# A sign bit made by another engine: converting 64-bit weights in an attention and gated-MLP kernel

## The chip, the cores and the metric

The kernel runs on one core of one Trainium2 chip, in one launch. The metric is the device time of one execution in microseconds. A core has five engines with a queue each: TensorE (PE in the profile, its weight loads are PEld), VectorE (DVE), ScalarE (ACT), GpSimd (POOL) and SyncE (SP), which issues nearly all DMAs here. An engine works through its queue in order and waits on semaphores.

## The reference

Banded attention with sinks, and then a gated MLP over its output. The attention has 4 batches, 8 heads, 768 positions and head size 64:

```python
scores = scale * np.matmul(q, k.transpose(0, 1, 3, 2))
keep = is_sink | in_window            # key < 4, or 0 <= query - key < 128
a = softmax(np.where(keep, scores, -1e9));  out = np.matmul(a, v)
h = np.maximum(x @ w_in, 0.0)         # x: heads side by side, 512 wide; w_in: 512 x 1024
conv = sum(conv_w[k] * shift(h, k - 1) for k in range(3))     # along positions, per channel
return (h * sigmoid(conv)) @ w_out    # w_out: 1024 x 512
```

q, k and v are 32-bit floats. The three weights w_in, conv_w and w_out are scaled by a 64-bit number when they are made and so arrive as 64-bit floats, which the kernel has to turn into 32-bit ones on the chip.

## The kernel before, in words

Each pair of heads of a batch is a group; there are 16 groups, and a group has six tiles of 128 queries. One step of the main loop (line 734) is one tile: scores (line 378 for the first batch, in plain f32; lines 381 and 382 for the others, as high and low parts), the mask and row minimum on VectorE (line 577), the exponential on ScalarE (line 580), the sum and its reciprocal on VectorE (lines 583 and 584), the scaling of the probabilities on GpSimd (line 586), their transposes on TensorE (line 603 for the first batch), a copy to SBUF by ScalarE, and the product with v (lines 655 and 678). Once three tiles of a half are done, the result goes to the MLP's input as a high and a low part (lines 389 and 390).

The MLP of a batch is cut into units of 256 positions by 128 hidden channels. A unit has twelve products into `ph` (line 204), the gate (lines 211 to 230, on ScalarE, VectorE and GpSimd), and products into `po` (line 239). Units are filled in between the attention steps; the first batch's begin in the middle of its attention, since the MLP needs x.

The weights are loaded in 128x512 tiles: eight of w_in, eight of w_out, and one small tile (24x128) of conv_w, the taps. `WHEN` (line 35) and line 757 convert one tile per step from step 2 to step 18. `load` fetches the raw pairs of 32-bit words; `narrow` makes a 32-bit float of each pair; `split` makes of it a high part H on GpSimd (line 130) and a low part L on VectorE (line 131), as TensorE multiplies in a reduced form of f32. For the taps `narrow` writes into a part of a buffer `hb`, and there is no split.

In `narrow`, ScalarE multiplies the upper word, read as a float, by 2^-112 (line 118), which takes the difference of the two exponent biases out. The result `low` has the sign in its top bit, then three zero bits, then the wanted bits. VectorE shifts it left by 3 (line 121), which drops the sign, or-s in the top three bits of the lower word (line 122), and or-s the sign back in (line 123). `w` and `low` are both of tag `st`, which has three buffers and which the output tiles of line 244 use too. Line 120 lets ScalarE's instruction wait for an exponential of a recent step.

The order of each engine's queue is not written out by hand: the program is traced, and a planner orders it by priority along a timeline of its own with costs it assumes (line 938). The attention steps get a higher priority (line 731), TensorE's instructions of the attention go through `c.pin`, and some waits are added by `follow` (line 47).

Of the kernel before, what the change touches and what calls it, by code (L numbers as in the profile page):

```python
# [14 lines left out]
ALU = mybir.AluOpType  # L15
# [23 lines left out]
def f(ap):  # L39
    return ap.bitcast(F32)  # L40
# [6 lines left out]
def follow(c, ins, other, reason):  # L47
    c.tc.add_manual_dep(ins.ins, other.ins.name, mybir.DependencyInfo(mybir.DependencyClass.Sync, mybir.DependencyReason.DATA),
                        reason=reason)
# [17 lines left out]
class Moe:  # L67
# [41 lines left out]
    def narrow(self, raw, to=None):  # L109


        if raw.dtype == F32:
            return raw
        nc, (rows, n) = self.c.nc, raw.shape[0:2]
        w = self.temp("st", 512, 3)[0:rows, 0:n] if to is None else to
        low = self.temp("st", 512, 3)[0:rows, 0:n]
        lo, hi, wi, li = raw[:, :, 0], raw[:, :, 1], w.bitcast(I32), low.bitcast(I32)
        first = nc.scalar.mul(low, f(hi), 2.0 ** -112)
        if len(getattr(self.c, "exps", [])) > 1:
            follow(self.c, first, self.c.exps[-2], "late")  # L120
        nc.vector.tensor_scalar(wi, li, 3, None, ALU.logical_shift_left)
        nc.vector.scalar_tensor_tensor(out=wi, in0=lo, scalar=29, in1=wi, op0=ALU.logical_shift_right, op1=ALU.bitwise_or)  # L122
        nc.vector.scalar_tensor_tensor(out=wi, in0=li, scalar=-0x80000000, in1=wi, op0=ALU.bitwise_and, op1=ALU.bitwise_or)  # L123
        return w

    def split(self, raw, parts, at):
# [815 lines left out]
```

## Time and profile before

| | |
|---|---|
| runs before | 474.14 us median of 3 (473.42 to 474.23) |
| profiled execution | 473.48 us, of which the span is 471.8 us |
| granted TensorE clock | 0.997 of full speed |
| PE | 444.6 us (94%) |
| PEld | 388.3 us (82%) |
| DVE | 339.0 us (72%), 1190 instructions |
| ACT | 321.3 us (68%) |
| POOL | 281.3 us (60%), 557 instructions |

Busy times are unions over the span, from the first to the last instruction. An average over the span hides that the stages differ: what matters is which engine is full in the stage that a change touches, and what waits for it there. The end of a matmul is modelled, and matmuls are pipelined, so a duration of one of them is longer than the time it takes from the engine.

### The profile page before, as it was taken

How to read it: one execution, taken by the hardware profiler on the slowest of the kernel's cores; microseconds unless marked ns; L12 is line 12 of the kernel's file. 1: busy time of each engine (PE TensorE's matmuls, PEld its weight loads, DVE VectorE, ACT ScalarE, POOL GpSimd, SP SyncE). 2: the span in 40 equal slices, each digit the busy share in tenths (PEclk: the TensorE clock that was granted, in tenths of full speed). 3: DMA queues.
4: the chain of work that ended last, by engine and by line, in shares of the span. 5: the costliest groups of instructions: out<-in, count | busy, mean ns of one | idle time of the engine just before them, and what ended most of it. 6: DMA issues, size and time to landing. Idle time of an engine off the chain costs nothing.

```text
span 471.8 us, 10560 instructions
## 1 busy us (share of the span) xinstructions
PE 444.6 (94%) x3181; PEld 388.3 (82%) x3181; DVE 339.0 (72%) x1190; ACT 321.3 (68%) x1027; POOL 281.3 (60%) x557
## 2 busy tenths in 40 slices
PE   3898989898899999999999999999999999999994
PEld 3576768697798988898989898988989898998982
DVE  4799999758858668786766859685767663665562
ACT  4989957768867868785867767675857654554542
POOL 3474786626858658676755757667656671445340
PEclk9999999999999999999999999999999999999998
DMA  6888674388667472655273655545250101000001
GB/s 140 219 229 251 183 201 107 81 199 203 167 153 179 137 175 68 161 146 133 61 192 81 166 119 134 143 120 124 71 141 15 46 1 46 0 23 24 24 24 53
DMA packets 105851, 55.91 MB, mean 119 GB/s; under 512 B 83072, under 2 KB 98712, under 8 KB 105784
## 3 DMA queue, kind: packets, MB, share of 16 engines
q1 hardware_dynamic: 105640, 55.00, 45.5%
q8 instruction: 28, 0.46, 0.4%
q14 instruction: 39, 0.32, 0.2%
q10 hardware_dynamic: 144, 0.13, 0.1%
HBM read 28.17 MB, written 6.29 MB: 73 GB/s over the span
## 4 chain that ended last, share of the span: by engine, by line
PE 75%; DVE 11%; ACT 4%; POOL 3%; DMA 2%; issue 2%; DVEq 0%; POOLq 0%; ACTq 0%
PE ph L204 26%; PE po L239 25%; PE px L655 7%; PE sc L382 3%; PE sc L381 3%; PE pts L617 3%; PE px L678 2%; DVE stm L122 2%; PE tq L305 1%; PE tk L331 1%; DVE stm L123 1%; DMA kk<-bk 1%; DMA raw<-in_q_dram 1%; DVE roomH L577 1%; DVE roomL L577 1%
## 5 line engine op out<-in xcount | busy, mean ns | idle before, releaser
L239 PE MATMUL po<-woH,g 128*128 128x512 f32 x384 | 138.2, 405 | 1.5 <-POOL g L226 0.8
L204 PE MATMUL ph<-xH,wiH 128*128 128x258 f32 (+1 forms) x384 | 110.7, 288 | 0.0
L204 PE MATMUL ph<-xL,wiH 128*128 128x258 f32 (+1 forms) x384 | 109.6, 286 | 0.0
L204 PE MATMUL ph<-xH,wiL 128*128 128x258 f32 (+1 forms) x384 | 109.1, 284 | 0.0
L226 POOL TENSOR_SCALAR g<-t 128x256 fp32r<-128x256 f32 x94 | 44.3, 472 | 74.5 <-DVE t L219 50.6
L586 POOL TENSOR_SCALAR pe<-pe,sm 128x132 f32<-128x132 f32 (+1 forms) x144 | 62.8, 447 | 37.7 <-DVE sm L584 19.2
L239 PEld LDWEIGHTS po<-woH,g 128*128 128x128 f32 x384 | 69.4, 189 | 13.2 <-POOL g L226 1.7
L227 POOL TENSOR_TENSOR g<-t,g 128x256 fp32r<-128x256 f32 x94 | 74.5, 793 | 5.8
L239 PE MATMUL po<-woL,g 128*128 128x512 f32 x192 | 76.1, 396 | 0.0
L216 DVE SCALAR_TENSOR_TENSOR t<-hb,cw,t 128x256 f32<-128x256 f32 x96 | 53.8, 560 | 29.4 <-ACT t L215 28.9
L204 PEld LDWEIGHTS ph<-xH,wiL 128*128 128x128 f32 x384 | 72.8, 190 | 2.2
L204 PEld LDWEIGHTS ph<-xH,wiH 128*128 128x128 f32 x384 | 72.7, 189 | 2.0
L204 PEld LDWEIGHTS ph<-xL,wiH 128*128 128x128 f32 x384 | 72.7, 189 | 1.6
L580 ACT ACTIVATE pe<-pe,sm 128x132 f32<-128x132 f32 (+1 forms) x144 | 58.2, 406 | 14.4 <-DVE sm L577 12.8
L218 ACT ACTIVATE t<-t 128x256 f32<-128x256 f32 x96 | 40.1, 418 | 36.3 <-DVE t L217 35.9
L219 DVE SCALAR_TENSOR_TENSOR t<-t,hb 128x256 f32<-128x256 f32 x96 | 48.3, 504 | 15.1 <-ACT t L218 14.3
L215 ACT ACTIVATE t<-hb,cw 128x256 f32<-128x256 f32 x96 | 49.0, 511 | 12.4 <-POOL g L227 10.1
L217 DVE SCALAR_TENSOR_TENSOR t<-hb,cw,t 128x256 f32<-128x256 f32 x96 | 54.4, 567 | 4.0 <-POOL pe L586 0.5
L211 ACT ACTIVATE hb<-ph 128x258 f32<-128x258 f32 (+1 forms) x96 | 36.8, 384 | 17.4 <-PE ph L204 13.9
L577 DVE CUSTOM_DVE_ANT_0 pe<-sc,m 128x132 f32<-128x132 f32 (+1 forms) x144 | 39.8, 287 | 7.7 <-PE sc L382 6.9
L381 PE MATMUL sc<-kk,X 128*128 128x260 f32 (+1 forms) x144 | 42.3, 304 | 1.5 <-issue 1.1
L655 PE MATMUL px<-pT,vraw 128*64 128x128 f32 (+1 forms) x512 | 43.0, 317 | 0.0
(161 smaller groups left out, 896.1 us busy)
## 6 DMA issues: line engine op xcount, KB each, us to landing
X<-bq SPq DMA_DIRECT2D x96, 96.0 KB
vraw<-in_v_dram SPq DMA_DIRECT2D x16, 384.0 KB
out_dram<-stm SPq DMA_DIRECT2D x23, 256.0 KB
kk<-kk SPq DMA_DIRECT2D x24, 198.0 KB
raw<-in_k_dram SPq DMA_DIRECT2D x24, 192.0 KB
raw<-in_q_dram SPq DMA_DIRECT2D x24, 192.0 KB
kk<-bk SPq DMA_DIRECT2D x48, 96.0 KB
raw<-in_q_dram SPq DMA_DIRECT2D x16, 96.0 KB
```

The lines of the kernel that those rows point to most:

```text
L204: self.latest = nc.tensor.matmul(u.h[:, 0:W], w[:, cc, ff * P:(ff + 1) * P], x[:, cc, t0:t1], start=(i == 0), stop=(i == len(prods) - 1))
L215: nc.scalar.mul(a, prev, cw[:, 0, ff:ff + 1])
L216: nc.vector.scalar_tensor_tensor(out=e, in0=this, scalar=cw[:, 1, ff:ff + 1], in1=a, op0=ALU.mult, op1=ALU.add)
L217: nc.vector.scalar_tensor_tensor(out=a, in0=nxt, scalar=cw[:, 2, ff:ff + 1], in1=e, op0=ALU.mult, op1=ALU.add)
L219: nc.vector.scalar_tensor_tensor(out=a, in0=e, scalar=1.0, in1=this, op0=ALU.add, op1=ALU.mult)
L227: nc.gpsimd.tensor_tensor(out=u.g[:, 1], in0=a, in1=f(u.g[:, 0]), op=ALU.subtract)
L239: ins = nc.tensor.matmul(po[:, 0:c.DM], u.g[:, a, tt * P:(tt + 1) * P], w[:, ff, :], start=(ff == 0 and i == 0), stop=(ff == NFF - 1 and i ...
L381: self.c.pin(self.nc.tensor.matmul(pc, X[:, j, u, :], kk[:, j, lo:hi], start=True, stop=False))
L577: nc.vector.tensor_tensor_reduce(out=pe[:, j, cols], in0=pc[:, P - at:SW][:, cols], in1=mk, op0=ALU.add, op1=ALU.min, scale=1.0, scalar=3. ...
L580: exp = nc.scalar.activation(pe[:, j, cols], pe[:, j, cols], AF.Exp, bias=sm[:, j:j + 1], scale=-1.0, accum_out=sm[:, 2 + 2 * j:3 + 2 * j])
L586: nc.gpsimd.tensor_scalar(pe[:, j, cols], pe[:, j, cols], sm[:, 8 + j:9 + j], 1.0, ALU.mult, ALU.mult)
L655: ins = nc.tensor.matmul(px[h][D * j:D * j + D, P * at:P * at + n], s.v[:, j, kt, :], pT, start=(h not in open_), stop=False, skip_group_c ...
```

## The change

The product of `low` with zero is a zero with the sign of `low`. GpSimd makes it, into `w`, in place of VectorE's shift. VectorE's first remaining instruction or-s the top three bits of the lower word into `w`, as before; its second shifts `low` left by 3 and or-s the result in.

```diff
         first = nc.scalar.mul(low, f(hi), 2.0 ** -112)
         if len(getattr(self.c, "exps", [])) > 1:
             follow(self.c, first, self.c.exps[-2], "late")
-        nc.vector.tensor_scalar(wi, li, 3, None, ALU.logical_shift_left)
+        nc.gpsimd.tensor_scalar(w, low, 0.0, 1.0, ALU.mult, ALU.mult)
         nc.vector.scalar_tensor_tensor(out=wi, in0=lo, scalar=29, in1=wi, op0=ALU.logical_shift_right, op1=ALU.bitwise_or)
-        nc.vector.scalar_tensor_tensor(out=wi, in0=li, scalar=-0x80000000, in1=wi, op0=ALU.bitwise_and, op1=ALU.bitwise_or)
+        nc.vector.scalar_tensor_tensor(out=wi, in0=li, scalar=3, in1=wi, op0=ALU.logical_shift_left, op1=ALU.bitwise_or)
         return w
```

Before, the order of a tile is ScalarE (118), VectorE (121, 122, 123), GpSimd (130), VectorE (131). After, it is ScalarE (118), GpSimd (121), VectorE (122, 123), GpSimd (130), VectorE (131).

## Rows read from the trace of the kernel before

**Rows 1.** Busy time by stretch: start:end, length, each engine's busy us (and instructions).

```profile
core 0: us, PE busy (x) PEld busy (x) DVE busy (x) ACT busy (x) POOL busy (x), PEclk, DMA share, GB/s
...
12.00:88.00 76.00, 66.40 (x466) 52.35 (x465) 72.19 (x221) 61.31 (x187) 48.36 (x70) 1.00 0.69 187
88.00:100.00 12.00, 11.76 (x99) 10.62 (x99) 6.84 (x23) 9.21 (x27) 5.71 (x11) 1.00 0.68 159
100.00:200.00 100.00, 96.66 (x741) 85.13 (x741) 73.80 (x329) 76.67 (x275) 67.68 (x147) 1.00 0.64 158
200.00:400.00 200.00, 200.00 (x1462) 178.42 (x1461) 140.77 (x518) 136.10 (x452) 128.23 (x259) 1.00 0.41 103
```

**Rows 2.** Chain of waits, 12 to 88 us: shares of this stretch by line.

```profile
by line: DVE stm L122 11.1%; DVE stm L123 8.2%; issue 7.4%; DMA raw<-in_q_dram 6.4%; DVE roomH L577 5.6%; DVE roomL L577 5.4%; DVE woL L131 4.9%; ACT roomL L580 4.6%; DVE stm L121 4.1%; DVE xL L390 3.7%; PE sc L378 3.5%; DVE wiL L131 3.5%; 
```

**Rows 3.** Waits of TensorE, 12 to 88 us: total us, times, longest.

```profile
PE sc L378 <- DVE sm L577: 3.0, 4, 1.1
PE pts L603 <- POOL roomL L586: 1.8, 3, 0.8
PE pts L603 <- POOL roomH L586: 1.1, 2, 0.6
```

**Rows 4.** VectorE by line, 12 to 88 us: count, busy us, mean ns, idle before.

```profile
L123 DVE SCALAR_TENSOR_TENSOR stm<-stm,stm 128x512 int32<-128x512 int32 x16 | 11.7, 732 | 0.0
L121 DVE TENSOR_SCALAR stm<-stm 128x512 int32<-128x512 int32 x16 | 9.6, 598 | 0.5 <-ACT stm L118 0.3
...
L121 DVE TENSOR_SCALAR hb<-stm 24x128 int32<-24x128 int32 x1 | 0.2, 206 | 0.0
```

**Rows 5.** Durations of lines 121 and 123, ns: least, median, most.

```profile
L121 DVE TENSOR_SCALAR stm<-stm x16: 405/540/886, 13.7 to 80.4; 128x512 int32<-128x512 int32 x16
...
L123 DVE SCALAR_TENSOR_TENSOR stm<-stm,stm x16: 664/680/1193, 16.8 to 84.3; 128x512 int32<-128x512 int32 x16
```

**Rows 6.** Timeline of GpSimd and VectorE: start us, us, instruction.

```profile
57.98 0.62 POOL L130 TENSOR_SCALAR wiH<-stm 128x512 fp32r<-128x512 f32 x1 [0.65 <-DVE sm L584]
...
76.86 0.61 POOL L130 TENSOR_SCALAR woH<-stm 128x512 fp32r<-128x512 f32 x1
...
58.00 0.89 DVE L121 TENSOR_SCALAR stm<-stm 128x512 int32<-128x512 int32 x1
58.80 0.41 DVE L577 CUSTOM_DVE_ANT_0 roomL<-sc,roomH 128x260 f32<-128x260 f32 x1
...
76.87 1.14 DVE L122 SCALAR_TENSOR_TENSOR stm<-wo6r,stm 128x512 int32<-128x512 int32 x1
```

**Rows 7.** Chain of waits in order of time: start us, us, what.

```profile
39.51 0.76 POOL roomL L586
...
58.22 0.58 issue
...
66.45 0.79 POOL g L226
...
68.86 1.52 POOL roomL L586 x2
...
86.48 1.71 POOL roomH L586 x2
```

**Rows 8.** GpSimd by line, 12 to 88 us: count, busy us, mean ns, idle before.

```profile
L586 POOL TENSOR_SCALAR roomH<-roomH,sm 128x260 f32<-128x260 f32 (+1 forms) x24 | 18.0, 761 | 5.4 <-DVE sm L584 3.2 <-ACT hb L211 0.8 <-PE px L678 0.8
L586 POOL TENSOR_SCALAR roomL<-roomL,sm 128x260 f32<-128x260 f32 (+1 forms) x18 | 12.5, 705 | 2.2 <-PE px L678 2.2
L130 POOL TENSOR_SCALAR wiH<-stm 128x512 fp32r<-128x512 f32 x8 | 5.3, 659 | 7.2 <-DVE sm L584 4.3 <-DVE sm L583 2.9
L130 POOL TENSOR_SCALAR woH<-stm 128x512 fp32r<-128x512 f32 x8 | 5.2, 656 | 7.1 <-DVE stm L123 6.5 <-DVE sm L583 0.6
```

**Rows 9.** Waits of VectorE, 12 to 88 us: total us, times, longest.

```profile
DVE wiL L131 <- POOL wiH L130: 0.4, 1, 0.4
```

**Rows 10.** Waits of SyncE's queue, whole span: total us, times, longest.

```profile
SPq L106 <- DVE stm L122: 20.2, 10, 5.1
```

## The prediction

> **What bounds the kernel now.** I read the busy time by stretch first. From 200 to 400 us TensorE has no gap, and it is 97 to 98% busy between 88 and 200 us; in the stretch from 12 to 88 us it works only 66.4 of 76 us, while VectorE works 72.2 (95%), ScalarE 61.3 and GpSimd 48.4 [rows 1]. All seventeen weight conversions lie in that stretch. TensorE's later work is the same in amount and nearly without gaps, so what the stretch loses or wins should arrive at the end almost unchanged.
>
> The chain of waits says the same by line: from 12 to 88 us the conversion's own VectorE lines 122, 123, 131 and 121 are its largest items, and line 121, the one that goes, holds 4.1% of 76 us, or 3.1 us [rows 2]. TensorE's own idle time there, 9.6 us, is ended by VectorE's row minimum (3.0 us) and by GpSimd's scaling of the exponentials (1.8 + 1.1 us and smaller ones) [rows 3]. So the change takes work from the bound of this stretch and gives it to an engine that TensorE also waits for.
>
> **What is removed.** Line 121 runs sixteen times on 128x512, 9.6 us, and once for the taps, 0.2 us: 9.8 us of VectorE [rows 4]. It takes 405 ns at best and 886 at worst [rows 5]; the worst ones run beside GpSimd: at 58.00 it takes 0.89 us beside a GpSimd instruction that started at 57.98 [rows 6]. The chain books part of such a delay as "issue" (0.58 us at 58.22, until the next VectorE instruction at 58.80) [rows 6, 7]. I add that to the 3.1: line 121 is worth 3.7 us of the chain, 0.38 of its 9.8 us. The other 6.1 us run where another chain is equally late, and I give them nothing; the upper bound, if all of them counted, is the 9.6 us that TensorE idles.
>
> **What stays.** Two VectorE instructions with two inputs remain per tile. The new second one (shift by 3, then or) has the operands and shape of the old line 123, 732 ns on average [rows 4], so its price doesn't change. ScalarE's line 118 and all DMAs are the same.
>
> **What is added.** GpSimd gets a product of a 128x512 f32 tile with two constants, sixteen times and once on 24x128. Line 130 is that operation on that shape: 659 and 656 ns [rows 8]; only its output type differs. That makes 16 x 0.657 + about 0.2 for the taps = 10.7 us, and GpSimd goes from 48.4 to about 59 of 76 us. It stays below the other engines, but its queue is in order, and it scales the exponentials for which TensorE's transposes wait. The chain stays in GpSimd for long three times: 0.76 us at 39.51, 3.9 us from 66.45 to 70.38 and 1.7 us at 86.48, together 6.4 us [rows 7]. If 10.7 us spread over 48.4 us of GpSimd work, these visits get 10.7 x 6.4 / 48.4 = 1.4 us longer. Below that lies 0 (no new product in front of any of them), above it 2.0 us (one of 0.66 in each). I take the 1.4.
>
> **New waits.** The product waits for ScalarE's word, and its output buffer is one that VectorE's last instruction on an earlier tile has read, since three "st" buffers serve two live tiles. Behind it on GpSimd stand the next scalings, the gate's g and the next tile's H. The first VectorE instruction of a tile now waits for the product, and behind that stand the row minima of line 577, for which ScalarE's exponentials and TensorE's score buffers wait. Nearest to this wait is line 131, which already waits for GpSimd's line 130 in the same way: of sixteen, one waited visibly, 0.4 us [rows 9]. Sixteen more such waits would cost 0.4, on the chain 0.2 us. The lower end is 0, the upper the second rival below. SyncE is touched as well: it issued ten weight loads only after waiting for line 122 to free a raw buffer, 20.2 us in all, and the next q and k loads stand behind them [rows 10]. These waits now move with the product, by less than the 0.9 us per tile of the second rival, and the relief of VectorE moves them the other way; no weight load is among what ended TensorE's idle time, so I put them at 0.
>
> **Sharing.** More GpSimd work lies beside VectorE's two-input instructions. Line 123's mean lies 68 ns above its best, 664 [rows 4, 5]; for 33 such instructions and 10.7/48.4 = 22% more GpSimd work this is 0.5 us, 0.2 on the chain. Its lower bound is 0 (line 121 no longer collides with GpSimd at all, which could even hand a little back).
>
> The upper bound comes from one row: at 76.87 line 122 took 1.14 us beside a line 130 started at 76.86 [rows 6]; if line 122 costs alone what line 123 does at its median, 0.68, that is 0.46 too much, and seventeen times that would be 7.8 us, 3.0 on the chain. The Trainium skill (SBUF — State Buffer, "Who interferes with whom") says why that could be the rule: VectorE with two SBUF inputs and a reading GpSimd exclude each other, and the later one stands still to the end. By it the new product would be as bad a neighbour as line 130 is at 76.86 and the removed instruction was no worse a one; the third rival prices that. The trace agrees only in part: line 123's median, 680 ns, is nearly its best [rows 5], so most don't stand still.
>
> **The planner.** The program's order is planned anew from assumed costs, so neighbours may move. No row prices this; TensorE still idles 3.3 us between 100 and 200 us under the present plan [rows 1], and I take half of it, 1.7 us, as the size of a move either way, and 0 as its value.
>
> **Sum.** 3.7 - 1.4 - 0.2 - 0.2 = 1.9 us shorter. The profiled execution took 473.48 us with a span of 471.8; it would take 471.6. The median of the runs before, 474.14, lies 0.66 above it, so I forecast 474.1 - 1.9 = 472.2. With the planner's 1.7 its own range is 470.5 to 473.9.
>
> **Rivals.**
> 1. *All of VectorE's relief counts.* TensorE becomes the fullest engine of the stretch at the share VectorE has now, 95%: 66.4 / 0.95 = 69.9 instead of 76 us, 6.1 less, so 468.0. For it: TensorE holds 97% between 100 and 200 us with VectorE at 74% [rows 1]. Against it: then VectorE, ScalarE and GpSimd would all have to run at 84 to 89%, each waiting for the others.
> 2. *The slower one: the wait takes the place of the work.* VectorE's first instruction stands at the head of its queue while GpSimd first ends a scaling and then makes the product. GpSimd is busy 0.64 of the stretch, half a scaling is 0.36 us [rows 1, 8]: 0.23 + 0.66 = 0.89 us per tile, 14.2 in all against 9.8 saved, 4.4 us more, of which 0.38 or 1.7 us arrive: 475.8. It decides from a wait of 0.6 us per tile (9.8 / 17). For it: the product follows a ScalarE step and has to be ready before both VectorE instructions, where earlier only VectorE's own order counted. Against it: the sixteen instructions of line 131, nearly none of which waited.
> 3. *Sharing eats it.* Each product costs VectorE 0.46 us: 17 x 0.46 = 7.8 of the 9.8. The remaining 2.0 are worth 0.8 on the chain; less 1.4 and 0.2 this is 0.8 slower, 475.0, just inside what can't be told from no change.
> 4. *Line 121 is only half on the path*, a second chain through GpSimd's scaling being as late: 1.85 of the 3.7 us, less the same 1.8: no change, 474.1.
>
> **How the numbers follow.** Forecast 0.50, rivals in order 0.12, 0.20, 0.07, 0.11. A measurement here tells about 0.2% (0.95 us) from no change, so faster means below 473.2, slower above 475.1. The forecast's range reaches into "same" with a tenth of it. Faster: 0.45 + 0.12 = 0.57. Same: 0.05 + 0.11 + 0.04 of the third and 0.01 of the second = 0.21. Slower: 0.19 + 0.03 = 0.22. The range goes from 469.0 (it leaves out most of the first rival) to 475.8 (it leaves out half of the second): about 0.2 outside.
>
> **What would show it.** If I am right: VectorE's busy time falls by 9 to 10 us, GpSimd's rises by 10 to 11, and the stretch that holds the conversions ends about 2 us earlier, with TensorE's work after it as before; the new product takes 0.62 to 0.7 us. The second rival would show as VectorE's first conversion instruction waiting for GpSimd's product by several us in total; the third as line 122 and its successor at 0.9 us and more on average; the first as TensorE's idle time in the stretch falling by more than 5 us. The prediction is wrong if the line that waits longest for GpSimd is a VectorE one, or if the time moves although this stretch ends when it did.

## The result: 5.6 us slower, and where the trace shows it

The changed kernel takes 479.36 us (median of 4 runs, 479.25 to 480.59) and the kernel before, on the same chip, 473.78 (473.06 to 474.23): ratio 1.0117, 95% interval 1.0088 to 1.0146. I had forecast 1.9 us less; it is 5.6 us more. Times are medians, and one execution of the kernel with idle matmuls, 728.55 us at a clock of 0.56, is left out of its median. The profiled execution took 479.25 us, with a span of 477.5.

The page of the changed kernel, its span, busy times and granted clock:

```profile
span 477.5 us, 10602 instructions
...
PE 449.2 (94%) x3181; PEld 389.0 (81%) x3181; DVE 331.9 (69%) x1173; ACT 322.8 (68%) x1027; POOL 290.7 (61%) x574
...
PEclk9979999999999999999999999999999999999998
```

VectorE's work fell by 7.1 us, not by 9 to 10, GpSimd's rose by 9.4, and the clock has a dip in the third slice (24 to 36 us) that the kernel before does not have. Busy time by stretch, columns as in [rows 1]:

```profile
12.00:88.00 76.00, 66.36 (x453) 51.32 (x452) 64.50 (x197) 59.79 (x177) 56.15 (x84) 0.96 0.67 184
...
100.00:200.00 100.00, 95.55 (x719) 82.76 (x718) 72.83 (x315) 75.40 (x263) 62.13 (x138) 1.00 0.66 160
200.00:400.00 200.00, 200.00 (x1469) 177.85 (x1468) 141.14 (x532) 138.23 (x464) 132.44 (x268) 1.00 0.41 102
```

Against [rows 1], VectorE is relieved (72.2 to 64.5 us), and no engine took its place as the full one. TensorE is busy as long as before, but with 453 recorded instructions where it had 466, at a clock of 0.96: it worked more slowly and got less done (whether the clock is the cause of the loss is asked under "The half clock"). From 100 us on it is nearly as full as before, with 1.1 us more of idle time up to 200 us. The starts of the same work in both traces say when the loss is made: the last conversion's line 131 starts at 91.65 us instead of 86.62, and the 201st product into `po` at 243.8 instead of 238.8; the last one starts at 471.3 instead of 465.5. So 5 us are lost by the end of the conversions, and 5.8 in the end.

Where it begins is seen in a finer cut of the same view:

```profile
18.00:20.00 2.00, 1.86 (x12) 1.33 (x12) 1.65 (x10) 2.00 (x9) 2.00 (x4) 1.00 0.88 176
20.00:22.00 2.00, 1.38 (x10) 0.86 (x8) 1.82 (x4) 2.00 (x8) 2.00 (x4) 1.00 0.89 295
22.00:23.00 1.00, 0.41 (x2) 0.12 (x1) 0.26 (x3) 0.92 (x3) 1.00 (x3) 1.00 1.04 346
23.00:24.00 1.00, 0.00 (x0) 0.00 (x0) 0.76 (x1) 0.82 (x3) 1.00 (x3) 0.89 1.24 289
24.00:26.00 2.00, 1.22 (x3) 1.03 (x4) 0.90 (x7) 1.24 (x5) 1.92 (x5) 0.50 1.01 230
26.00:28.00 2.00, 2.00 (x8) 1.04 (x7) 1.76 (x6) 1.20 (x6) 0.34 (x3) 0.50 0.66 188
```

GpSimd has not one free moment from 18 to 24 us. My 59 of 76 us was an average over a stretch in which it is full at times. TensorE stands still between 23 and 24 us, and behind that it runs at half clock, 1.2 of 2.4 GHz, until 30.6 us (the next row, 28 to 30, has 0.50 too). The timeline of these microseconds (start us, us, instruction):

```profile
19.52 0.62 POOL L121 TENSOR_SCALAR stm<-stm 128x512 f32<-128x512 f32 x1
...
20.12 1.38 POOL L586 TENSOR_SCALAR roomH<-roomH,sm 128x260 f32<-128x260 f32 x2
20.18 0.96 DVE L122 SCALAR_TENSOR_TENSOR stm<-wi_1r,stm 128x512 int32<-128x512 int32 x1 [0.53 <-POOL stm L121]
...
22.59 0.62 POOL L130 TENSOR_SCALAR wiH<-stm 128x512 fp32r<-128x512 f32 x1
...
23.24 0.96 DVE L131 TENSOR_TENSOR wiL<-stm,wiH 128x512 fp32r<-128x512 f32 x1 [0.94 <-POOL wiH L130]
24.42 0.29 DVE L577 CUSTOM_DVE_ANT_0 roomH<-sc,m 128x128 f32<-128x128 f32 x1
...
24.78 2.10 PE L378 MATMUL sc<-kks,X 128*128 128x260 f32 x4 [1.92 <-DVE sm L577]
...
28.56 0.62 POOL L121 TENSOR_SCALAR stm<-stm 128x512 f32<-128x512 f32 x1
28.63 1.08 DVE L131 TENSOR_TENSOR wiL<-stm,wiH 128x512 fp32r<-128x512 f32 x1 [0.26 <-POOL wiH L130]
```

The product at 19.52 pushes the scalings back; H (line 130) comes late behind them, VectorE stands 0.94 us for it with line 131 at the head of its queue, the row minimum of line 577 stands behind that, and TensorE's scores wait 1.92 us for the minimum. In the trace of before the same four score products wait 0.98 us and take 1.15 instead of 2.10:

```profile
22.31 0.62 POOL L130 TENSOR_SCALAR wiH<-stm 128x512 fp32r<-128x512 f32 x1 [0.75 <-DVE sm L584]
...
22.96 0.69 DVE L131 TENSOR_TENSOR wiL<-stm,wiH 128x512 fp32r<-128x512 f32 x1 [0.41 <-POOL wiH L130]
...
23.92 1.15 PE L378 MATMUL sc<-kks,X 128*128 128x260 f32 x4 [0.98 <-DVE sm L577]
```

H itself starts only 0.28 us later after the change; the other half of VectorE's longer wait (0.94 against 0.41) is that VectorE comes to it 0.25 us earlier. Line 131 then takes 0.96 instead of 0.69 us, and TensorE's scores start 0.86 us later. The waits of VectorE from 12 to 88 us (total us, times, longest), those that GpSimd ends:

```profile
DVE woL L131 <- POOL woH L130: 2.3, 3, 1.1
DVE wiL L131 <- POOL wiH L130: 2.3, 4, 0.9
DVE stm L122 <- POOL stm L121: 1.8, 2, 1.3
...
DVE roomH L577 <- POOL roomH L586: 0.7, 1, 0.7
```

Together, with 0.2 us for the taps, 7.3 us, against 0.4 in [rows 9]. And line 131 itself became slower. Its rows and the product's in the two traces by line, first before, then after:

```profile
L131 DVE TENSOR_TENSOR wiL<-stm,wiH 128x512 fp32r<-128x512 f32 x8 | 5.7, 713 | 0.4 <-POOL wiH L130 0.4
L131 DVE TENSOR_TENSOR woL<-stm,woH 128x512 fp32r<-128x512 f32 x8 | 5.6, 696 | 0.0
```

```profile
L131 DVE TENSOR_TENSOR wiL<-stm,wiH 128x512 fp32r<-128x512 f32 x8 | 8.1, 1013 | 2.3 <-POOL wiH L130 2.3
L131 DVE TENSOR_TENSOR woL<-stm,woH 128x512 fp32r<-128x512 f32 x7 | 7.2, 1033 | 2.3 <-POOL woH L130 2.3
...
L121 POOL TENSOR_SCALAR stm<-stm 128x512 f32<-128x512 f32 x16 | 10.5, 656 | 0.0
```

Line 131 starts when H is ready, and the next instruction in GpSimd's queue is now often the next tile's product, as at 28.56 and 28.63 above. In 12 of 16 cases line 131 runs beside a product; 11 of these take 1.085 to 1.10 us, where it takes 0.68 alone. Beside scalings it took 0.69 (at 18.13, beside one) and 0.96 (at 23.24, beside two). So 12 x 0.4 us = 4.9 us of VectorE. With 7.3 - 0.4 us of new waits this is 11.8 us given back for 9.8 us saved [rows 4]. That balance of VectorE's time does not by itself make a loss in the kernel's time, as the next section shows: without a product VectorE waits for H and the scalings too, 3.4 us from 12 to 92 us, and nothing is lost.

### The profile page after: what moved, and what is told of

It reads as the page before. It is cut to its first block, busy times and chain, and to the rows that moved or that the text cites. A ratio compares the mean times of both kernels' runs of the same rounds, so it can differ in the third digit from the quotient of the medians.

```text
span 477.5 us, 10602 instructions
## 1 busy us (share of the span) xinstructions
PE 449.2 (94%) x3181; PEld 389.0 (81%) x3181; DVE 331.9 (69%) x1173; ACT 322.8 (68%) x1027; POOL 290.7 (61%) x574
## 4 chain that ended last, share of the span: by engine, by line
PE 75%; POOL 8%; DVE 6%; ACT 5%; issue 2%; DMA 2%; SPq 0%; DVEq 0%; POOLq 0%; ACTq 0%
PE ph L204 26%; PE po L239 25%; PE px L655 7%; PE pts L617 3%; PE sc L381 3%; PE sc L382 3%; PE px L678 2%; POOL roomH L586 2%; POOL roomL L586 2%; PE tk L331 1%; PE tq L305 1%; PE sc L378 1%; ACT X L288 1%; POOL stm L121 1%; DVE stm L122 1%
## 5 line engine op out<-in xcount | busy, mean ns | idle before, releaser
L226 POOL TENSOR_SCALAR g<-t 128x256 fp32r<-128x256 f32 x94 | 42.4, 452 | 67.2 <-DVE t L219 48.0
L227 POOL TENSOR_TENSOR g<-t,g 128x256 fp32r<-128x256 f32 x94 | 73.4, 782 | 5.3
L216 DVE SCALAR_TENSOR_TENSOR t<-hb,cw,t 128x256 f32<-128x256 f32 x96 | 53.5, 557 | 32.4 <-ACT t L215 31.8
L580 ACT ACTIVATE pe<-pe,sm 128x132 f32<-128x132 f32 (+1 forms) x144 | 58.2, 406 | 17.2 <-DVE sm L577 16.3
L219 DVE SCALAR_TENSOR_TENSOR t<-t,hb 128x256 f32<-128x256 f32 x96 | 49.5, 517 | 17.9 <-ACT t L218 16.9
L217 DVE SCALAR_TENSOR_TENSOR t<-hb,cw,t 128x256 f32<-128x256 f32 x96 | 51.5, 538 | 4.5 <-DVE t L216 0.5
L621 POOL TENSOR_SCALAR_AFFINE_SELECT pT<-pT 128x256 f32<-128x256 f32 x60 | 27.2, 454 | 31.9 <-ACT pT L619 31.4
L655 PE MATMUL px<-pT,vraw 128*64 128x128 f32 (+1 forms) x512 | 44.3, 322 | 0.0
```

The costliest lines, as they stand in the source:

```text
L216: nc.vector.scalar_tensor_tensor(out=e, in0=this, scalar=cw[:, 1, ff:ff + 1], in1=a, op0=ALU.mult, op1=ALU.add)
L217: nc.vector.scalar_tensor_tensor(out=a, in0=nxt, scalar=cw[:, 2, ff:ff + 1], in1=e, op0=ALU.mult, op1=ALU.add)
L219: nc.vector.scalar_tensor_tensor(out=a, in0=e, scalar=1.0, in1=this, op0=ALU.add, op1=ALU.mult)
L226: nc.gpsimd.tensor_scalar(u.g[:, 0], a, 1.0, 1.0, ALU.mult, ALU.mult)
L227: nc.gpsimd.tensor_tensor(out=u.g[:, 1], in0=a, in1=f(u.g[:, 0]), op=ALU.subtract)
L580: exp = nc.scalar.activation(pe[:, j, cols], pe[:, j, cols], AF.Exp, bias=sm[:, j:j + 1], scale=-1.0, accum_out=sm[:, 2 + 2 * j:3 + 2 * j])
```

## The experiments

Three questions: what does each part of the change cost by itself; is it the place or the number of the products; what is the half clock worth. All ratios are against runs of the kernel before on the same chip; the runs come from several chips, on which the kernel before took 473.8 to 474.8 us.

**The relief alone.** The sign is left out, so GpSimd makes no product and VectorE has one short operation less; its first remaining one also reads one tensor instead of two.

```diff
-        nc.gpsimd.tensor_scalar(w, low, 0.0, 1.0, ALU.mult, ALU.mult)
-        nc.vector.scalar_tensor_tensor(out=wi, in0=lo, scalar=29, in1=wi, op0=ALU.logical_shift_right, op1=ALU.bitwise_or)
+        nc.vector.tensor_scalar(wi, lo, 29, None, ALU.logical_shift_right)
```

> The sign bit is left out altogether: VectorE's first instruction writes the three low bits alone, the second shifts and or-s; no GpSimd product. This is VectorE's relief without its price. Theories A and B: faster than before by the 1.5 to 4 us that line 121 was on the chain, 470 to 472.3, line 131 at 0.70 us. Theory C: if the plan alone decides, it may be as slow as 476 to 480 although there is less work.

Measured 474.08 us, ratio 1.0001 (0.9979 to 1.0024). Busy time by stretch of this kernel:

```profile
12.00:88.00 76.00, 66.14 (x469) 54.48 (x467) 61.91 (x205) 60.42 (x185) 46.13 (x72) 0.96 0.68 187
```

VectorE has 10.3 us less to do in the stretch than in [rows 1], the last line 131 starts at 71.4 us, 15 us earlier, and TensorE got through 469 instructions instead of 466. Less work on VectorE was worth nothing measurable, and the time lies outside all the ranges I had given. One thing clouds it: the clock of 0.96 comes from half clock from 18.8 to 22.2 and from 42.7 to 46.1 us, which the kernel before does not have. So the zero is the relief less whatever this costs.

**The load alone.** Sixteen products into H's place, which line 130 overwrites; VectorE keeps its three operations and waits for none of them.

```diff
+        if to is None:
+            nc.gpsimd.tensor_scalar(self.spare, low, 0.0, 1.0, ALU.mult, ALU.mult)
...
+        self.spare = H
         w = self.narrow(raw)
```

> The kernel before, with GpSimd's sixteen products added as pure load: they read the same words and write into H's place, which line 130 overwrites later; VectorE keeps its three instructions and waits for none of them. If GpSimd's fullness is what costs (scalings and H come late): 476 to 479. If the product as a step in front of VectorE is what costs: 473.5 to 475.

Measured 477.71 us, 1.0096 (1.0063 to 1.0129): 3.5 us. TensorE's waits for the scalings, 12 to 92 us:

```profile
PE pts L606 <- POOL roomH L589: 3.9, 5, 1.3
PE pts L606 <- POOL roomL L589: 1.4, 2, 0.8
PE pt L606 <- POOL roomL L589: 1.0, 1, 1.0
```

That is 6.3 us; the same three rows of before make 1.4 + 1.8 + 0.9 = 4.1 (most of it stands in [rows 3]). GpSimd's load by itself makes more than half of the loss, by the medians. But the way is another than in the changed kernel: there TensorE waits less for the scalings than before (1.7 + 0.6 + 0.3 = 2.6 us, 12 to 92 us) and longer for the row minima of line 577 (4.2 us against 3.0). And the execution traced here is the fastest of eight, 476.10 us.

**The hop alone.** The kernel without the sign, with a product of one column, for which VectorE's first operation has to wait.

```diff
+        nc.gpsimd.tensor_scalar(w[:, 0:1], low[:, 0:1], 0.0, 1.0, ALU.mult, ALU.mult)
         nc.vector.tensor_scalar(wi, lo, 29, None, ALU.logical_shift_right)
```

> The kernel without a sign bit (VectorE's two instructions), but VectorE's first one has to wait for a GpSimd product of one column (128x1) of the tile: the step without the load. If GpSimd's fullness is what costs: within 1 us of the kernel without a sign, 473.5 to 475. If the step in front of VectorE is what costs: 476 to 479, and VectorE waits 3 us or more for the product.

Measured 476.79 us, 1.0053 (1.0025 to 1.0081); without the hop it was 474.08, so the hop costs 2.7 us by the medians (2.5 by the ratios). VectorE's longest wait in it, 12 to 92 us:

```profile
DVE stm L122 <- POOL stm L121: 4.8, 4, 2.5
```

**Load and hop without the relief.** The product stands in front of the three old VectorE operations.

```diff
         nc.gpsimd.tensor_scalar(w, low, 0.0, 1.0, ALU.mult, ALU.mult)
+        nc.vector.tensor_scalar(wi, li, 3, None, ALU.logical_shift_left)
```

> GpSimd makes the product and VectorE keeps all three instructions of before (the shift then overwrites the product): the price without the relief. Theory A: the same GpSimd queue, gap and clock drop, and a fuller VectorE: 480 to 484. Theory B: line 131 at about 1.05 us as well, 481 to 483. Theory C: may be as fast as before, 473 to 476.

480.86 us, 1.0148 (1.0103 to 1.0192): 7.0 us, against 3.5 + 2.7 = 6.2 from the two parts. The changed kernel, which differs from this one by the relief alone, loses 5.6: so beside the product the relief is worth 1.4 us by the medians, though the intervals overlap.

**The same product on ScalarE.** There it has no scaling and no H to push back. The output lacks the sign here: its relative error is 30.84, the same as that of the kernel that leaves the sign out.

```diff
-        nc.gpsimd.tensor_scalar(w, low, 0.0, 1.0, ALU.mult, ALU.mult)
+        nc.scalar.mul(w, low, 0.0)
```

> The product with zero is made by ScalarE, right behind its line 118, not by GpSimd; the rest as changed. Theory A2: VectorE waits for GpSimd as little as before (under 1 us in 12 to 88 us), line 131 takes 0.70 us again, GpSimd's scaling is on time; ScalarE has 11 us more in this stage: 472 to 475 if no gap lets the clock fall, up to 3 us more if one does. Theory B2 (any further hop in front of VectorE's two instructions costs the relief): 477 to 480.

475.04 us, 1.0023 (1.0002 to 1.0044): 0.8 us. Line 131 of this kernel, and VectorE's wait for the product, 12 to 92 us:

```profile
L131 DVE TENSOR_TENSOR wiL<-stm,wiH 128x512 fp32r<-128x512 f32 x8 | 5.6, 706 | 1.9 <-POOL wiH L130 1.9
```

```profile
DVE stm L122 <- ACT stm L121: 4.1, 4, 1.2
```

VectorE waits for the product even longer than in the changed kernel (4.1 against 1.8 us), and line 131 waits 3.0 us for H (1.9 and 1.1), where I had expected under 1. Yet nearly all of the loss is gone, and line 131 is back at 0.7 us. These rows are from the slowest of ten executions, 477.45 us, 2.4 above the median. By the medians it is GpSimd that makes the difference.

**Two misses at making room.** Copying H on ScalarE (`nc.scalar.copy(H, w)` in line 130) should free GpSimd, in the changed kernel and, as a control, in the one before:

> GpSimd makes the sign product, but the high part H (line 130) is a copy by ScalarE: GpSimd has as many conversion instructions as before the change, ScalarE sixteen more, the sign product still stands in front of VectorE. Theory A2, if GpSimd's load is what counts: no long waits of VectorE for GpSimd, 472 to 476. If the hop to GpSimd in front of VectorE is what counts: waits of VectorE for the product stay at 2 us or more, 477 to 480.

> The kernel before with its high part H copied by ScalarE and not by GpSimd: the opposite of the load, 10.5 us less on GpSimd, 11 us more on ScalarE. If GpSimd's fullness already costs in the kernel before: 472 to 473.5. If it only costs with the product on top: 474 to 476, as ScalarE gets fuller.

478.89 us (1.0085, 1.0057 to 1.0113) and 475.05 us (1.0024, 0.9995 to 1.0053). Taking as much work off GpSimd as the product adds is not enough: the first of them is 3.8 us above its control, as forecast for the hop, and VectorE now waits 7.0 us for the product (7 times, 2.8 at most). Taking the product from the raw upper word, `f(hi)` instead of `low`, so that it need not wait for ScalarE:

> GpSimd multiplies the raw upper word, not ScalarE's scaled one, so that the product waits for the load alone and not for ScalarE; GpSimd's count is that of the changed kernel. If the load of GpSimd counts: as slow as the change, 477 to 481. If waiting for ScalarE in GpSimd's queue counts: 474 to 476.

479.34 us, 1.0110 (1.0076 to 1.0144). No part of the step on ScalarE ahead of the product is seen in the time.

**Is it a new order of the program?** Every change makes the planner place everything anew. This kernel changes only the small taps tile (`if to is not None:` ahead of the new lines, the old ones otherwise):

> Only the taps tile (24x128) is converted in the new way; the 16 large tiles and one small go the old way, so GpSimd gets one product of 0.7 us and VectorE is relieved of one short operation. If load and steps make the loss: 473.5 to 475, no difference from before. If any new plan loses, whatever it adds: 476 to 480, with a gap of TensorE of over 1.5 us somewhere that the kernel before does not have.

474.02 us, 0.9988 (0.9967 to 1.0010). This new plan, and the one product in it, lose nothing; it is one plan of many.

**Place or number.** The new path for the last eight tiles only, `if self.done >= 9:`, and for the first nine, `if self.done < 9:`.

> The sign product on GpSimd only for the last eight tiles (second half of w_in, second half of w_out); the first nine conversions keep VectorE's three instructions. Theory A (GpSimd's queue is full in the first 30 us; VectorE waits for its products, TensorE gets a gap there and then runs at half clock for 6.4 us): no clock drop at 24 to 30 us, TensorE clock 0.997, time 472 to 474, at most that of before. Theory B (line 131 collides with the next tile's product and takes 1.09 instead of 0.70 us, wherever it runs): eight such instructions, half of the loss, about 476.5. Theory C (the new plan of the order, not the operation): no relation to the number of tiles, anything from 473 to 480.

> The sign product on GpSimd only for the first nine conversions (first half of w_in, taps, first half of w_out); the last eight keep VectorE's three instructions. Theory A: the whole loss stays, 478.5 to 480, with a clock drop at 24 to 30 us. Theory B: half of the loss, about 476.5, no need of a clock drop. Theory C: anything from 473 to 480.

479.41 us (1.0109, 1.0063 to 1.0155) and 480.79 us (1.0143, 1.0102 to 1.0184): half the products cost as much as all, or more. Theories A and B fell: A gave 472 to 474 for the first, B 476.5 for both. In the first most of the loss arises from 50 us on, and the trace shows GpSimd again (timeline; the line numbers are 5 higher, 122 is the product, 135 H, 591 the scaling):

```profile
50.03 3.51 POOL L591 TENSOR_SCALAR roomH<-roomH,sm 128x260 f32<-128x260 f32 x4
...
53.52 0.79 POOL L135 TENSOR_SCALAR wiH<-stm 128x512 fp32r<-128x512 f32 x1
54.29 0.77 POOL L122 TENSOR_SCALAR stm<-stm 128x512 f32<-128x512 f32 x1
54.51 1.09 DVE L136 TENSOR_TENSOR wiL<-stm,wiH 128x512 fp32r<-128x512 f32 x1
55.05 2.17 POOL L591 TENSOR_SCALAR roomH<-roomH,sm 128x260 f32<-128x260 f32 x2
...
57.25 0.27 ACT L614 COPY sk<-roomH 128x96 f32<-128x96 f32 x1 [2.25 <-POOL roomH L591]
...
57.57 0.31 PE L615 MATMUL tk<-ident,sk 128*96 128x128 f32 x1 [2.84 <-ACT sk L614]
```

H and the product stand ahead of two scalings that take 2.17 us; ScalarE and TensorE wait for them, 2.25 and 2.84 us. So I took a single worst place for the cause, and tried the two tiles around the gap at 23 us, `if self.done in (1, 2):`

> The new path only for two tiles, those whose products stand at 19.5 and 25.6 us in the changed kernel, around TensorE's gap at 23 us. If one worst place decides: 476.5 to 479, with the gap of 1.5 us or more near 23 us and half clock behind it. If the loss is a sum over the 17 tiles (5.6 us for 17, so 0.33 us each): 474.4 to 475, without that gap.

473.27 us, 0.9985 (0.9961 to 1.0009): no loss seen. That theory fell. The next question was whether the products have to follow closely: the first four (`self.done < 4`), every other tile (`self.done % 2 == 1`, eight in all) and every third (`self.done % 3 == 1`, six).

> The new path only for the first four tiles in a row, whose products stand within 14 us of each other. If delays pile up where products follow closely: 476.5 to 480, with TensorE's gap of over 1.5 us near 23 us. If the loss is a sum (some 0.33 us for each product): 475.5 to 476.2. If a few products are harmless wherever they stand: 473 to 475.

> The new path for every other tile, eight products in all, as many as in e1_late. If closeness decides: below 475.5, since VectorE has a tile in the old way, with no wait, between two in the new one. If the number decides: 477 to 480, as e1_late (479.4).

> The new path for every third tile, six products. If closeness decides: 473 to 475, no slower than before and perhaps 1 us faster, as e13_two (473.3). If the loss is a sum: 476 to 477.

475.35 us (1.0006, 0.9981 to 1.0031), 474.31 us (0.9994, 0.9969 to 1.0019) and 475.13 us (1.0020, 0.9995 to 1.0046). Eight products spread over every other tile cost nothing that can be told, eight in a row 5.5 us, and the first eight with the taps 6.9. Four in a row are not told from no change either, although that kernel has a gap of 1.72 us at 23.0; but its interval reaches to 1.5 us, so a sum of 0.33 us for each of the four is not excluded by it, nor by the six (to 2.2 us). It is by the spread eight, where a sum would make 2.6 us and the interval ends at 0.9, and narrowly by the two (0.7 and 0.4). So in these kernels the loss came with a long row of tiles that are all converted the new way. VectorE in the kernel with every other tile, 12 to 88 us, its line 131 (there 136), and its waits for GpSimd:

```profile
L136 DVE TENSOR_TENSOR wiL<-stm,wiH 128x512 fp32r<-128x512 f32 x8 | 6.9, 858 | 0.5 <-POOL wiH L135 0.4
L136 DVE TENSOR_TENSOR woL<-stm,woH 128x512 fp32r<-128x512 f32 x8 | 6.8, 847 | 1.1 <-POOL woH L135 1.1
```

```profile
DVE woL L136 <- POOL woH L135: 1.1, 2, 0.6
DVE roomH L582 <- POOL roomH L591: 0.7, 1, 0.7
...
```

With two smaller ones, 0.6 and 0.4 us, 2.8 us of waits instead of 7.3, and five products beside a line 131 instead of twelve. The old-style tiles in between, which wait for no product, leave room to make up a delay. That is my reading; the traces show less waiting, but not that the room is the reason.

**The half clock.** Eight idle matmuls `ident` x `ident` in TensorE's gap keep it at work there:

```diff
+            for i in range(WARM):
+                last = nc.tensor.matmul(warm[:, 0:P], c.ident, c.ident, start=True, stop=True)
+                if i == 0:
+                    follow(c, last, c.sunk[-2], "warm")
+            pin, c.pin = c.pin, lambda ins: follow(c, ins, last, "warm")
```

> The changed kernel with eight products of the identity with itself (128x128 f32, result never read) on TensorE, put in the place where TensorE stood still for 1.9 us at 22.9 us; nothing else is taken away. Theory A2 (the loss has two parts: some 3 us because TensorE ran at half clock from 24 to 30 us after that gap, and some 2.5 us of VectorE waiting for GpSimd): no half-clock stretch between 24 and 31 us, 476 to 477.5. Theory B2 (the half clock hides behind VectorE, which bounds this stage; all the loss is VectorE's): 479 to 480 whether or not the clock falls.

477.88 us, 1.0068 (1.0040 to 1.0095), between the two forecasts. Then once more, side by side with the changed kernel:

> The changed kernel as it is, for comparison with e15_warm_again on the same chip: 479 to 480 by every theory, gap near 23 us, half clock from 24 us to about 30 us.

> The changed kernel with eight idle matmuls where TensorE stood still. If the half clock costs something by itself: 1 to 3 us below e14_after_again, with a granted clock nearer to that of the kernel before. If it costs nothing, because GpSimd and VectorE set the end of the stage: within 0.7 us of e14_after_again.

479.45 us (1.0108, 1.0072 to 1.0145) without, 477.52 us (1.0070, 1.0044 to 1.0097) with them. Busy time by stretch, first without, then with the idle matmuls:

```profile
20.00:24.00 4.00, 1.61 (x11) 0.97 (x9) 3.03 (x7) 3.17 (x11) 4.00 (x7) 1.00 1.01 291
24.00:28.00 4.00, 3.49 (x18) 2.46 (x20) 2.65 (x14) 2.93 (x12) 2.25 (x7) 0.71 0.86 211
28.00:32.00 4.00, 3.89 (x29) 2.91 (x27) 3.45 (x11) 1.40 (x4) 4.00 (x7) 0.86 0.75 200
```

```profile
20.00:24.00 4.00, 3.39 (x27) 2.79 (x26) 2.71 (x7) 2.98 (x11) 4.00 (x8) 1.00 0.99 292
24.00:28.00 4.00, 3.72 (x32) 2.85 (x32) 2.58 (x11) 2.75 (x10) 2.56 (x7) 1.00 0.92 222
28.00:32.00 4.00, 2.65 (x22) 1.94 (x18) 3.41 (x10) 2.27 (x9) 3.00 (x6) 1.00 0.79 210
```

With the clock at 1.00 throughout, 1.9 us come back by the medians (1.5 in the first trial, against 479.36), though the intervals of the two kernels overlap. That this is the price of the half clock is not shown: the idle matmuls also make the program's order another. Two pairs of executions, each of one kernel in one order, speak against it. The changed kernel had half clock from 23.8 to 30.6 us in its first trace, and only from 25.7 to 29.1 in this one, whose row for the whole stretch is:

```profile
12.00:88.00 76.00, 64.64 (x453) 50.47 (x453) 64.40 (x197) 59.60 (x177) 56.17 (x84) 0.98 0.67 184
```

TensorE gets the same 453 recorded instructions done as at 0.96 and only stands idle 1.7 us longer; the last line 131 starts 0.14 us earlier, at 91.51 us, and the 201st product into `po` at 243.8 in both. Likewise the kernel with idle matmuls had half clock from 73.3 to 76.7 us in the first trial's trace and none in the second; its 41st product into `po` starts at 100.4 us in both. So half clock that was absent gave back almost nothing. What the last 3.4 us of it behind the gap cost, no pair tells. In any case this kernel still loses 3.0 us by the medians, and its traced execution, with no half clock at all in the conversions, took 476.57 us, 2.0 above the median of before.

No version beats both kernels: the best, with two tiles, is not told from the kernel before.

## Why the prediction was wrong

It had the sign wrong, and the time lies 3.6 us above its range (469.0 to 475.8). Its sum was 3.7 - 1.4 - 0.2 - 0.2. The experiments give for the same terms:

| step | predicted | measured |
|---|---|---|
| What is removed | 3.7 saved | 0 (+0.2 by the medians, within 1.1 either way); 1.4 saved beside the product, by the medians |
| What is added (load on GpSimd) | 1.4 lost | 3.5 lost by the medians (3.0 to 6.1 by the ratio's interval) |
| New waits (hop) | 0.2 lost | 2.7 lost by the medians |
| Sharing | 0.2 lost | not by itself; 4.9 us of VectorE on line 131 |
| The planner | 0 | 0.5 saved by the medians, not told from 0 (the taps tile alone) |

0 + 3.5 + 2.7 = 6.2 us by parts, 5.6 measured; 7.5 us off the forecast, of which the first step makes 3.7 (2.3 if the relief is worth 1.4). That the parts come near the whole is in part luck: each is its own plan, with an interval of some 2 to 3 us.

- **What bounds the kernel now**: failed. I read VectorE's 95% in the stretch [rows 1] as the bound and gave it the length of the stretch. With 61.9 instead of 72.2 us of VectorE the time is the same, in a kernel with two stretches of half clock. I also misread [rows 2]: the row minimum of line 577 holds 5.6 + 5.4 = 11.0% of the chain, as much as the conversion's largest line and more than each of the others. The busy share was that of an engine filled with work that nobody was waiting for: the conversions ran ahead of TensorE's need for them by a wide margin, and could end 15 us earlier without any effect that was measured.
- **What is removed**: failed, for the same reason. The share of line 121 on the chain [rows 2] was true of that one chain. Where the line was taken out, other chains were as late, as the fourth rival said of half of it.
- **What is added**: the kind was right, the price not. The product takes 0.656 us as forecast (0.657), the small one for the taps 0.72 instead of 0.2. I spread 10.7 us evenly over GpSimd's queue and counted three visits of the chain [rows 7]. But the products and H come in bursts with the scalings, and in a burst GpSimd is full (18 to 24 us). What stands behind is then late. How late differs: H only 0.28 us at 22.59, but ScalarE and TensorE more than 2 us at 57 in the kernel with the last eight tiles.
- **New waits**: failed most in kind. I took the one wait of line 131 [rows 9] as the model of a wait. Sixteen old waits were short since GpSimd was free when H came due; the products took that away in part. Now line 131 waits 4.6 us in seven places. But waiting alone is not losing: in the kernel without a product it waits 2.8 us for H too, and the time stays that of before.
- **Sharing**: looked for in the wrong place. Line 123 stayed at 724 ns (732 before), while line 131, which I had not looked at, went from 0.70 to over 1.0. The Trainium skill (SBUF — State Buffer, "Who interferes with whom") has VectorE with two SBUF inputs and a reading GpSimd exclude each other, the later one blocked to the end. For line 131 beside the product the trace agrees in direction: the product starts 0.07 us earlier (28.56 and 28.63), and line 131 takes 0.4 us longer; blocked to the product's end it would be about 0.55. Beside a scaling it agrees only in part: at 18.07 a scaling of 128x260 started 0.06 us before line 131, and it was the scaling that took long, 1.01 us where others take 0.37, while line 131 took 0.69; at 23.24, again 0.06 us behind a scaling, line 131 took 0.96. In the prediction I let line 123's median decide against this rule.
- **The second rival** had the side right (475.8, chance 0.20), of the size a third (1.7 of 5.6 us), and the place wrong: VectorE's line 122 waits for the product 2.0 us in all, not 14.2. What waits and slows is line 131, through H and the next tile's product.
- **What would show it**: the sign I named for being wrong, that the line that waits longest for GpSimd is a VectorE one, is there: line 131 with 4.6 us. SyncE's queue behaved as forecast: its loads wait 17.2 us for line 122 instead of 20.2 [rows 10].
- **Half clock**: not in the prediction at all. What it is worth stays open: the kernel that avoids it is 1.9 us faster by the medians, but two executions of the changed kernel, one with half as much of it, kept the same pace.

So the step that failed is the first, a saving of 3.7 us where 0 to 1.4 was measured, together with the price of the product on GpSimd, 1.6 us forecast and about 6 measured. That the product's place on GpSimd makes the loss is shown (5.6 us there, 0.8 on ScalarE); by which of load, hop and the slower line 131 is not, as each was measured in a kernel with its own order.

Open: why a row of eight loses 5.5 us or more and a row of four none that can be told. The number of products beside a line 131 goes with it only roughly (12 in the changed kernel, 6 with the last eight tiles, 5 with every other, 1 with the first four), and the load alone loses 3.5 us with one. With GpSimd's load taken back to that of before, the product still loses 3.8 us against its control. Each kernel is also one plan; a plan's own chance and the noise move the medians by up to 1.3 us in the five kernels with six products or fewer, or eight spread.

## What to carry to other kernels

An engine at 95% is the bound of a stretch only if its work is waited for: ask for each of its long items who needs the result and when, and price its removal by that, not by its share of one chain. Before moving work to an engine with a low average, look at that engine in windows of one or two microseconds around the places where others wait for it; in-order queues charge a moved instruction to whatever stands behind it, and a wait that was short because the engine was idle does not stay short. Where an instruction of one engine slows one of another, as the product here slowed line 131 from 0.68 to 1.09 us, look at which instruction of the other engine will stand beside the new one at every tile, as a fixed order repeats the collision.

## What the runs showed of the hardware

- TensorE's clock fell to half (0.50, 1.2 GHz) after single pauses in this first stretch: 1.92 us without work at 22.9 us, then half clock from 23.8 to 30.6 us although it was busy all of 26 to 30. In another execution of the same kernel it fell after 1.93 us at 22.6, but only from 25.7 to 29.1. In the kernel with the last eight tiles it fell after 2.84 us at 54.7, and not after 2.15 us at 33.2. A pause was not always followed by a fall: with the first four tiles, none came after 1.72 us at 23.0, and one after 1.76 and 1.19 us at 30.6 and 32.9.
- Where two executions of the changed kernel in the same order can be compared, 3.4 us less of half clock gave back 0.14 us at 91 us and 0.02 at 243.
- VectorE's two-input operation on 128x512 took 0.68 us alone, and 1.09 beside GpSimd's 128x512 product that had started 0.07 us earlier and kept its 0.62. Beside GpSimd's 128x260 scaling, started 0.06 us earlier, it took 0.69 in one place, where the scaling took 1.01 instead of 0.37, and 0.96 in another.
- ScalarE's product with 0.0 did not keep the sign of its input: the output's relative error, 30.84, is that of the kernel without the sign. GpSimd's product kept it.
